# One VectorE call per convolution tap over all three thirds of the channels, in a kernel that fuses a seven-tap convolution with a GELU feed-forward block

## The chip, the cores and the metric

The kernel runs on one core of a Trainium2 chip. The metric is the device time of one execution in microseconds (us); the kernel before took 670.76 us in the median of three runs (670.53 to 673.35). TensorE (PE) multiplies matrices, VectorE (DVE) and ScalarE (ACT) do elementwise work, GpSimd (POOL) and SyncE (SP) mostly start transfers. Each engine has an instruction queue of its own and works it off in order. Between engines, and between two instructions of one engine that depend on each other, order is kept by semaphores only: an instruction adds to a semaphore when it has finished, and another waits until the semaphore has reached a number.

## The reference

The input is `x` of 8 x 4096 tokens with 192 channels. Each channel is convolved along the sequence with a causal filter of seven taps; the 24 channels of a head share a filter, which is a softmax over seven weights. The result goes through a feed-forward block of width 2048 with exact GELU:

```
out[b,s,h,g] = sum over k of softmax(weight[h])[k] * x_pad[b, s+k, h, g]      # 7 taps
h   = out @ w_in                        # 192 -> 2048
y   = gelu(h) @ w_out                   # 2048 -> 192
```

## The kernel before, in words

**Tiling.** The 32768 tokens are taken in two halves, which sit on partitions 0 to 63 and 64 to 127. Each half has 35 batches: six of 256 tokens, then 29 of 512 (`WS`). The 192 channels lie on 64 partitions in three *thirds*: channel 3i+p is row i of third p. So a convolution tap of a 512-token batch works on 128 partitions x 3 x 512 elements, that is 1536 a partition, and of a 256-token batch on 768.

**The way of batch n.** SP loads it into `xin`. VectorE transposes it into `xT` (`trans`, L729), channels on partitions. Then VectorE runs the taps: for each token, `acc = acc + x shifted by k * weight k` in float32 (`conv`, L757 scalar_tensor_tensor; tap 0 is a plain multiplication, L750), and the last tap writes bfloat16 into `xc`. Batches 0 and 1 (`PC`) get their convolution from TensorE instead. TensorE multiplies `xc` by `w_in` (`mm1`, L999) in 16 slices (8 for a 256-token batch), ScalarE puts GELU on each slice (L904) into `gT`, and TensorE multiplies that by `w_out` one batch later, between the slices of the next batch's `mm1` (L1077; L1143 in the batches named below). VectorE transposes the result into `osb` (L370, L537), and SP stores it.

**Calls of a tap.** Before the change each tap is two VectorE calls, s = 0 over the first two thirds (1024 elements) and s = 1 over the last third (512). Each tap reads what the tap before wrote. With two calls, the one that a call depends on is always the last but one on the queue, and the wait on `S_CV` is for that one (`idx - 1`).

**Batches in K0.** In most batches (4, 5, 6 and all from 9 on whose number less three is not in `ST`) ScalarE computes tap 0 in three instructions, one per third (`first_tap`, L872, 512 elements each). They are placed in ScalarE's queue before GELU slices 7, 10 and 12 of batch n-2 (`TAPS`; slices 2, 3 and 5 for batch 6). VectorE's first call of such a batch is tap 1, and each of its two calls waits on `S_K0` for the thirds that it reads.

**Batches in ST.** Every third batch from 9 to 33 (`ST`) has its second product computed by a scheme with fewer multiplications. It needs sums of GELU outputs (`st_add`: S1 at L473, S3 at L475, Dn at L478, S4 at L481), which VectorE makes while it convolves later batches, and combinations of the products (`st_post`, L510 to L525). TensorE's work for batch m in `ST` is a list of small units between the `mm1` slices of batch m+1 (`mm2_s`, L1143). The unit called P4 waits on `S_DP` for the first `st_post` call, here called *post0*: it subtracts what ScalarE has copied out, so that the bank can be accumulated into.

**The order on VectorE.** For each batch from 2 on `plan` lists its transpose and its conv calls, and the transpose of batch n+1 among them where that is a K0 batch. All other VectorE work (the sums, the post steps, the evacuations) is in a list `side` with a key (batch, position); a side operation goes out before the first plan operation whose position is not below its key. Positions count the calls of a tap, two each. For batch m in `ST`, the keys that matter here fall into batch m+2's list: S1 part 2 at position 1; S1 part 3, two evacuations, S3 and Dn at position 5; S4 at position 6; post0 at position 11. They come from these lines:

```
            "S1": [(1, 9, 0), (2, 0, 0), (2, 1, 0), (2, 5, -1)],
            "S3": [(2, 5, 1)],
            "Dn": [(2, 0, 2), (2, 5, 2)],
            "S4": [(2, 0, 4), (2, 6, 0)],
            "post": [(2, 11, 0), (3, 0, 0), (3, 2, 0), (3, 6, 0), (3, 9, 0)],
```

**Loads and buffers.** SP issues the load of a batch behind the store of an earlier one, which waits for three evacuations by VectorE. `xT`, `acc` and `xc` have two buffers each; GpSimd copies the six tokens of overlap between batches (`halo`, L652).

Of the kernel before, what the change touches and what calls it, by code (L numbers as in the profile page):

```python
# [11 lines left out]
def bass_lightweight_conv__then__act_gelu_exact_kernel(  # L12
# [8 lines left out]
    H, KS = weight.shape  # L21
# [7 lines left out]
    TB = 512  # L29
# [4 lines left out]
    PC = {0: 0, 1: 1}  # L34
# [5 lines left out]
    NP = D // 64  # L40
# [7 lines left out]
    HF = HX - (KS - 1)  # L48
    XW = HX + TB
# [69 lines left out]
    def ap(t, off, pat):  # L119
        return bass.AP(t, off, pat)  # L120

    with es:
# [52 lines left out]
        S_CV = sem("S_CV")  # L175
# [7 lines left out]
        S_K0 = sem("S_K0")  # L183
# [57 lines left out]
        def wait_pc(e, n, p):  # L241

            if n == 0:
                e.wait_ge(S_PCA, p + 1)
                if p >= 1:
                    e.wait_ge(S_PCE, p)
            else:
                e.wait_ge(S_PCA, len(PA) + 1)
                if p >= 1:
                    e.wait_ge(S_PCE, len(PV) + (0, 2, 5)[p])  # L250

        NCV = 2 * KS
        FQ = F // 8

        def part(q):
# [25 lines left out]

        def cvd(n):

            return sum(NCV - 2 * (m in K0) for m in range(n + 1) if m not in PC)


        def xin_at(n):
# [391 lines left out]
        @block.vector  # L679
        def _(v):  # L680
            v.memset(idb[:, :], 1.0).then_inc(S_MSET)
            v.wait_ge(S_WSB, 16)
            v.tensor_reduce(
                wmx[:, :], wsb[:, :], mybir.AxisListType.X, ALU.max, negate=True
            ).then_inc(S_PRO)
            v.wait_ge(S_ACTP, 2)
            v.tensor_scalar(wsm[:, :], wsm[:, :], 1e-9, None, ALU.add).then_inc(S_PRO)
            v.wait_ge(S_PRO, 2)
            v.reciprocal(wrc[:, :], wsm[:, :]).then_inc(S_PRO)
            v.wait_ge(S_PRO, 3)  # L690
            v.wait_ge(S_WNM, 1)
            v.tensor_scalar(  # L692
                wnm[0:H, 0:KS], wex[:, :], wrc[:, 0:1], None, ALU.mult
            ).then_inc(S_PRO)


            v.wait_ge(S_PRO, 4)
            v.transpose(wnt[:, :], wnm[:, :]).then_inc(S_PRO)
            v.wait_ge(S_PRO, 5)
            for q in range(4):  # L700
                v.transpose(  # L701
                    wcol[32 * q : 32 * q + 32, :],
                    ap(wnt, 4 * (q % 2), [[32, 32], [1, 4], [0, 8]]),
                ).then_inc(S_PRO)

            def trans(n, p):

                w = WS[n]
                if p == 0:
                    v.wait_ge(S_XP if n == 2 else S_XIN[n % NX], 64 if n == 2 else xin_at(n))  # L710
                    if n >= 2 and n - 2 in PC:
                        wait_pc(v, n - 2, NP - 1)
                    elif n >= 2:
                        v.wait_ge(S_CV, cvd(n - 2))
                    if n >= 2:
                        v.wait_ge(S_HALO, n)
                if n in PC:
                    out = ap(xT[n], p * XW + HX, [[NP * XW, 128], [1, w]])
                    src = ap(
                        xin[n % NX], p, [[TB // 32 * DQ, 128], [DQ, w // 32], [NP, 32]]  # L720
                    )
                else:
                    out = ap(xT[n % 2], HX, [[NP * XW, 128], [XW, NP], [1, w]])
                    src = ap(
                        xin[n % NX],
                        0,
                        [[TB // 32 * DQ, 128], [1, NP], [DQ, w // 32], [NP, 32]],
                    )
                v.transpose(out, src).then_inc(S_TR)  # L729

            def conv(n, k, s):

                w = WS[n]
                h = int(n in K0)
                p0, pn = (0, 2) if s == 0 else (2, 1)
                if k == h and s == 0:
                    v.wait_ge(S_TR, trd(n))
                if k == 1 and s == 0:
                    v.wait_ge(S_HALO, n + 1)
                idx = cvd(n - 1) + 2 * (k - h) + s  # L740
                kt = KS - 1 - k
                if k == h and h:
                    v.wait_ge(S_K0, NP * K0[n] + p0 + pn)
                elif idx >= 2:
                    v.wait_ge(S_CV, idx - 1)
                src = ap(xT[n % 2], p0 * XW + HF + kt, [[NP * XW, 128], [XW, pn], [1, w]])
                wk = wcol[:, kt : kt + 1]
                a = ap(acc[n % 2], p0 * TB, [[NP * TB, 128], [TB, pn], [1, w]])
                if k == 0:
                    ins = v.tensor_scalar(a, src, wk, None, ALU.mult)  # L750
                else:
                    dst = a
                    if k == KS - 1:
                        dst = ap(xc[n % 2], p0 * TB, [[NP * TB, 128], [TB, pn], [1, w]])
                        if n >= 2 and s == 0:
                            v.wait_ge(S_MM1, SL0[n - 1])
                    ins = v.scalar_tensor_tensor(  # L757
                        dst, src, wk, a, op0=ALU.mult, op1=ALU.add
                    )
                ins.then_inc(S_CV)  # L760

            plan = []
            for n in range(2, NB):
                ops = [] if n in K0 else [("t", n, 0)]
                ops += [("c", n, k, q) for k in range(int(n in K0), KS) for q in range(2)]
                if n + 1 in K0:
                    ops[6 if n < 6 else 2 : 6 if n < 6 else 2] = [("t", n + 1, 0)]
                plan.append(ops)  # L770

            def run(op):
                if op[0] == "t":
                    trans(*op[1:])
                else:
                    conv(*op[1:])

            trans(0, 0)
            for p in range(1, NP):
                trans(0, p)  # L780
            dup(v, 0, 0)
            for j in PV:
                conv_out(v, 0, j)
            dup(v, 1, 0)
            dup(v, 1, 1)
            trans(1, 0)
            trans(1, 1)
            trans(1, 2)
            dup(v, 2, 0)
            for j in range(1, 3):  # L790
                conv_out(v, 1, j)
            dup(v, 2, 1)
            for j in range(3, len(pieces(1))):
                conv_out(v, 1, j)

            side = [((M0 + 2, 4 * g, 0), evac, v, M0 - 1, g) for g in range(NG[M0 - 1])]
            side += [((M0 + 1, 2 * k + 1, 0), weights, v, k) for k in range(6)]
            for n in range(M0, M1):
                todo = []
                if n not in ST:  # L800
                    todo = [(at, evac_t, n, j) for j, at in enumerate(at_ev(n))]
                else:
                    for name, ats in AT_ST.items():
                        for q, at in enumerate(ats):
                            if name == "post":
                                todo.append((at, st_post, n, q))
                            elif name == "ev":
                                todo.append((at, st_evac, n, q))
                            else:
                                todo.append((at, st_add, n, name, q if name != "S3" else ND))  # L810
                side += [((n + at[0], *at[1:]), op, v, *rest) for at, op, *rest in todo]
            for n in range(M1, NB):
                for g in range(NG[n]):
                    side.append(((n + 3, g, 0), evac_half, v, g, 0))
            side.sort(key=lambda q: q[0])
            for b in range(2, NB):
                for o, op in enumerate(plan[b - 2]):
                    while side and side[0][0][:2] <= (b, o):
                        side[0][1](*side[0][2:])
                        side.pop(0)  # L820
                    run(op)
            for q in side:
                q[1](*q[2:])

# [93 lines left out]
        def _(t):  # L918
# [43 lines left out]
            def mm1(n, i):  # L962
# [6 lines left out]
                if i == 0:  # L969
                    if n in PC:  # L970
                        wait_pc(t, n, NP - 2)
                    else:
                        t.wait_ge(S_CV, cvd(n) - 1)
                if n == 0:
                    for j in {0: (0, 1), 2: (2, 5), 4: (3,), 6: (4,)}.get(i, ()):
                        t.wait_ge(S_WIN[j], 16)
# [6 lines left out]
                if head:  # L983
                    todo.sort(key=lambda q: q[1] == NP - 1)
                for cc, p in todo:
                    if i == 0 and cc == 0 and p == NP - 1:
                        if n in PC:
                            wait_pc(t, n, p)
                        else:
                            t.wait_ge(S_CV, cvd(n))  # L990
                    for hf in range(2):
                        r = slice(64 * hf, 64 * hf + 64)
                        ch = chunk(n, hf, i * c + cc)
# [259 lines left out]
```

## Time and profile before

| what | us |
|---|---|
| median of three runs | 670.76 (670.53 to 673.35) |
| profiled execution, first to last instruction (span) | 669.2 |
| what the median has on top of the span | 1.56 |
| TensorE busy | 665.8 (99%) |
| VectorE busy, 703 instructions | 604.7 (90%) |
| ScalarE busy, 659 instructions | 587.8 (88%) |
| GpSimd busy | 91.9 (14%) |

The profile gives no other time of the profiled execution than its span, so the span stands for it. Times in the timelines count from the start of the span. In a timeline a row gives the start, the length, the engine, the line, what is written and read, and how many like instructions are merged into it; a row can also say how long the engine sat idle before it and what ended that. From the first ST batch to the last the pattern repeats: in the timeline TensorE's rows return after 61.3 us, which is three batches.

### The profile page before, as it was taken

The page shows a single profiled execution, that of the slowest core. Times are in us where ns is not written, and L with a number is a line of the kernel's source. Part 1 is how long each engine was busy: PE and PEld are TensorE (multiplying, and loading weights), DVE is VectorE, ACT ScalarE, POOL GpSimd, SP SyncE. Part 2 cuts the span into 40 slices and gives each one's busy share as a digit, 9 for nine tenths or more (in the row PEclk, how much of TensorE's full clock was granted, in tenths as well). Part 3 has the DMA queues.
Part 4 walks back from the last instruction along what each step waited for, and adds up shares of the span by engine and source line. Part 5 has one row for each costly group of instructions (what it writes and reads, how often), then busy time and mean ns, then how long its engine had stood idle before and what let it go on. Part 6 is the DMA issues. An engine that isn't in the chain of part 4 may idle for free.

```text
span 669.2 us, 27224 instructions
## 1 busy us (share of the span) xinstructions
PE 665.8 (99%) x12504; PEld 416.2 (62%) x12504; DVE 604.7 (90%) x703; ACT 587.8 (88%) x659; POOL 91.9 (14%) x115
## 2 busy tenths in 40 slices
PE   9999999999999999999999999999999999999998
PEld 8999655556555655655565556556555655565567
DVE  5989999899999999999999999999999999999633
ACT  8999988899988988898999889888989998898783
POOL 8020000030012003001300120030013001200300
PEclk9999999999999999999999999999999999999999
DMA  9535234273466047515634660485157346602423
GB/s 153 123 86 132 61 72 97 73 132 85 96 143 139 9 96 176 112 36 126 140 84 97 140 143 7 96 176 111 39 127 140 82 97 142 139 8 61 119 63 96
DMA packets 142786, 67.82 MB, mean 101 GB/s; under 512 B 127248, under 2 KB 140880, under 8 KB 142672
## 3 DMA queue, kind: packets, MB, share of 16 engines
q1 hardware_dynamic: 129136, 49.37, 33.0%
q0 software_dynamic: 12416, 16.13, 12.1%
q8 instruction: 98, 1.61, 1.0%
q10 hardware_dynamic: 1120, 0.59, 0.3%
q14 instruction: 16, 0.13, 0.1%
HBM read 28.31 MB, written 25.17 MB: 80 GB/s over the span
## 4 chain that ended last, share of the span: by engine, by line
PE 99%; ACT 0%; DVE 0%; DMA 0%; issue 0%; ACTq 0%
PE hp L999 49%; PE ob L1077 29%; PE ob L1143 13%; PE ob L1039 5%; PE ob L1199 1%; PE hp L1199 1%; PE ob L941 0%; DMA wsb<-in_weight_dram 0%; PE ob L999 0%; ACT dg L846 0%; DVE wcol L701 0%; ACT xc L237 0%; DVE wnm L692 0%; ACT osb L344 0%; ACT wex L833 0%
## 5 line engine op out<-in xcount | busy, mean ns | idle before, releaser
L904 ACT ACTIVATE gT<-hp 128x1024 bf16<-128x1024 f32 x510 | 518.2, 1023 | 68.3 <-PE hp L999 60.5
L999 PE MATMUL hp<-xc,win 64*64 64x512 bf16 (+2 forms) x6036 | 416.8, 366 | 0.1
L757 DVE SCALAR_TENSOR_TENSOR acc<-xT,wcol,acc 128x1024 f32<-128x1024 f32 (+1 forms) x330 | 299.6, 957 | 7.3 <-ACT acc L872 7.3
L999 PEld LDWEIGHTS hp<-xc,win 64*64 64x64 bf16 (+1 forms) x6036 | 190.6, 106 | 126.5 <-ACT xc L237 0.3
L1077 PE MATMUL ob<-gT,wout 64*64 64x512 bf16 x3648 | 248.6, 376 | 0.0
L1077 PEld LDWEIGHTS ob<-gT,wout 64*64 64x64 bf16 x3648 | 116.9, 118 | 83.3
L1143 PE MATMUL ob<-gT,wout 64*64 64x512 bf16 x864 | 109.3, 376 | 0.0
L1143 PE MATMUL ob<-sst,wst 64*64 64x512 bf16 x432 | 88.9, 376 | 0.0
L729 DVE STREAM_TRANSPOSE xT<-xin 128x1536 f32<-128x1536 f32 (+2 forms) x39 | 74.6, 1922 | 9.7 <-DMA xin<-in_x_dram 9.3
L652 POOL COPY xT<-xT 128x18 f32<-128x18 f32 x30 | 28.9, 964 | 330.9 <-DVE xc L757 171.3
L1143 PEld LDWEIGHTS ob<-gT,wout 64*64 64x64 bf16 x864 | 48.8, 118 | 25.2
L757 DVE SCALAR_TENSOR_TENSOR xc<-xT,wcol,acc 128x1024 bf16<-128x1024 f32 (+1 forms) x66 | 61.9, 960 | 0.3
L370 DVE STREAM_TRANSPOSE osb<-ob 128x512 f32<-128x512 f32 x57 | 47.6, 874 | 4.0 <-PE ob L1077 3.7
L455 POOL DMA_DIRECT2D sst<-gT x27 | 19.8, 733 | 175.1 <-ACT gT L904 175.1
L872 ACT ACTIVATE acc<-xT,wcol 128x512 f32<-128x512 f32 (+1 forms) x63 | 43.6, 693 | 0.0
L1039 PE MATMUL ob<-wout,gT 64*128 64x192 bf16 x768 | 41.0, 243 | 0.0
L1143 PEld LDWEIGHTS ob<-sst,wst 64*64 64x64 bf16 x432 | 36.2, 107 | 6.0
L1143 PE MATMUL ob<-gT,wst 64*64 64x512 bf16 x144 | 39.7, 376 | 0.0
L1039 PEld LDWEIGHTS ob<-wout,gT 64*128 64x128 bf16 x768 | 33.4, 94 | 4.8
L458 POOL DMA_DIRECT2D sst<-gT x27 | 33.1, 1227 | 8.0 <-DMA sst<-gT 7.9
L473 DVE TENSOR_TENSOR sst<-gT 128x1024 bf16<-128x1024 bf16 x36 | 24.9, 691 | 10.0 <-ACT gT L904 9.9
L1143 PE MATMUL ob<-sst,wout 64*64 64x256 bf16 x288 | 30.8, 269 | 0.0
(75 smaller groups left out, 268.2 us busy)
## 6 DMA issues: line engine op xcount, KB each, us to landing
out_dram<-osb SPq DMA_DIRECT2D x124, 192.0 KB, 3.4
xin<-in_x_dram SPq DMA_DIRECT2D x116, 192.0 KB, 4.2
sst<-gT POOLq DMA_DIRECT2D x54, 256.0 KB, 4.1
xin<-in_x_dram SPq DMA_DIRECT2D x18, 96.0 KB, 2.4
wout<-in_moe_w_out_dram POOLq DMA_DIRECT2D x4, 192.0 KB, 4.5
win<-in_moe_w_in_dram POOLq DMA_DIRECT2D x4, 96.0 KB, 4.1
win<-in_moe_w_in_dram POOLq DMA_DIRECT2D x2, 192.0 KB, 4.1
xin<-in_x_dram POOLq DMA_DIRECT2D x4, 96.0 KB, 3.9
```

Source lines behind the costliest of these rows:

```text
L370: v.transpose(osb_t(m, j), bank(BK[m][j])).then_inc(S_EV)
L458: e.dma_start(dst, src, accum_op=ALU.add).then_inc(S_AD[q], 16)
L473: ins = v.tensor_tensor(t(0), a(1, 0), a(1, 1), ALU.add)
L652: g.tensor_copy(dst, src).then_inc(S_HALO)
L729: v.transpose(out, src).then_inc(S_TR)
L757: ins = v.scalar_tensor_tensor(dst, src, wk, a, op0=ALU.mult, op1=ALU.add)
L872: a.activation(out=acc[n % 2][:, p * TB : p * TB + w], in_=ap(xT[n % 2], p * XW + HX, [[NP * XW, 128], [1, w]]), func=AF.Copy, scale=wcol[ ...
L904: a.activation(out=ap(gT[n % 2], i * c * 2 * w, dst), in_=ap(ob, 2 * TB, [[4 * TB, 128], *src[1:]]) if u < SL0[1] and u % 3 == 2 else ap(h ...
L999: ins = t.matmul(hbuf(u, slice(fo, fo + fw), o, w), ap(win, f1, [[NP * F, 64], [2, fw]]), xc[n % 2][r, p * TB : p * TB + w], start=(p == 0 ...
L1039: ins = t.matmul(bb[sub], gT[m % 2][r, c0 : c0 + 128], wout[r, CH[sub][i] * C : (CH[sub][i] + 1) * C], start=(ph == 0 and k == 0), stop=(p ...
L1077: ins = t.matmul(bank(BK[m][j], slice(64 * h, 64 * h + 64), w), ap(wout, 64 * hf * NF * C + CH[h][i] * C + j, [[NF * C, 64], [NP, 64]],), ...
L1143: ins = t.matmul(bank(BK[m][bk], slice(64 * cg, 64 * cg + 64), w), wt_, a[r, c0 : c0 + w], start=(e == mine[0]), stop=(e in (mine[-1], GRO ...
```

## The change

A tap becomes one VectorE call over all three thirds: 1536 elements (768 in the 256-token batches). `S_CV` now counts one per tap, and a tap waits for the call just in front of it. In a K0 batch the first call waits for all three of ScalarE's thirds. TensorE's first matmul of a batch waits for all three thirds of `xc`, where before it waited for two and took the third up later. Positions in `plan` still count two per tap, so that the keys of the side list keep their meaning, but nothing can go out between the two halves of a tap any more.

```
-        NCV = 2 * KS
+        NCV = KS
...
-            def conv(n, k, s):
+            def conv(n, k):
...
-                p0, pn = (0, 2) if s == 0 else (2, 1)
...
-                idx = cvd(n - 1) + 2 * (k - h) + s
+                idx = cvd(n - 1) + k - h
                 kt = KS - 1 - k
                 if k == h and h:
-                    v.wait_ge(S_K0, NP * K0[n] + p0 + pn)
-                elif idx >= 2:
+                    v.wait_ge(S_K0, NP * (K0[n] + 1))
+                elif k == 0 and idx >= 2:
                     v.wait_ge(S_CV, idx - 1)
-                src = ap(xT[n % 2], p0 * XW + HF + kt, [[NP * XW, 128], [XW, pn], [1, w]])
+                elif k > 0:
+                    v.wait_ge(S_CV, idx)
+                src = ap(xT[n % 2], HF + kt, [[NP * XW, 128], [XW, NP], [1, w]])
...
-                ops += [("c", n, k, q) for k in range(int(n in K0), KS) for q in range(2)]
+                ops += [("c", n, k) for k in range(int(n in K0), KS)]
                 if n + 1 in K0:
-                    ops[6 if n < 6 else 2 : 6 if n < 6 else 2] = [("t", n + 1, 0)]
+                    at = 3 if n < 6 else 1 + (n not in K0)
+                    ops[at:at] = [("t", n + 1, 0)]
...
+                    o += 1 + (op[0] == "c")
...
-                        t.wait_ge(S_CV, cvd(n) - 1)
+                        t.wait_ge(S_CV, cvd(n))
...
-                    if i == 0 and cc == 0 and p == NP - 1:
-                        if n in PC:
-                            wait_pc(t, n, p)
-                        else:
-                            t.wait_ge(S_CV, cvd(n))
+                    if i == 0 and cc == 0 and p == NP - 1 and n in PC:
+                        wait_pc(t, n, p)
```

## The prediction

> **What bounds the kernel now.** I read the page first: the engines' busy time, then the chain that ended last.
>
> ```profile
> PE 665.8 (99%) x12504; PEld 416.2 (62%) x12504; DVE 604.7 (90%) x703; ACT 587.8 (88%) x659; POOL 91.9 (14%) x115
> ...
> PE 99%; ACT 0%; DVE 0%; DMA 0%; issue 0%; ACTq 0%
> ```
>
> TensorE is busy for 99% of the span and alone makes up the chain; the granted clock is 9 tenths or more in every slice. No VectorE time saved can shorten this. The change can only matter if VectorE hands something over so late that TensorE stops. So I next read the groups by shape, for the price of a call, and the waits.
>
> ```profile
> L757 DVE SCALAR_TENSOR_TENSOR acc<-xT,wcol,acc 128x1024 f32<-128x1024 f32 x145 | 184.1, 1270 | 0.0
> L757 DVE SCALAR_TENSOR_TENSOR acc<-xT,wcol,acc 128x512 f32<-128x512 f32 x165 | 122.3, 741 | 6.8 <-ACT acc L872 6.8
> ```
>
> ```profile
> DVE acc L757 <- ACT acc L872: 7.3, 12, 1.8
> ```
>
> The two shapes of a tap differ by 0.53 us for 512 elements. The small one has idle time before it: it waits for ScalarE's last third of tap 0, which the large one did not need. VectorE's timeline at the tightest place that I found, batch m+2 behind ST batch m:
>
> ```profile
> 324.57 1.26 DVE L757 SCALAR_TENSOR_TENSOR acc<-xT,wcol,acc 128x1024 f32<-128x1024 f32 x1
> 325.75 0.69 DVE L473 TENSOR_TENSOR sst<-gT 128x1024 bf16<-128x1024 bf16 x1
> 326.35 3.80 DVE L757 SCALAR_TENSOR_TENSOR acc<-xT,wcol,acc 128x512 f32<-128x512 f32 x4
> 330.41 0.69 DVE L473 TENSOR_TENSOR sst<-gT 128x1024 bf16<-128x1024 bf16 x1 [0.25 <-ACT gT L904]
> 331.01 1.60 DVE L370 STREAM_TRANSPOSE osb<-ob 128x512 f32<-128x512 f32 x2
> 332.48 0.66 DVE L475 TENSOR_TENSOR sst<-gT 128x1024 bf16<-128x1024 bf16 x1
> 333.05 1.22 DVE L478 TENSOR_TENSOR sst<-gT,sst 128x2048 bf16<-128x2048 bf16 x1
> 334.18 0.74 DVE L757 SCALAR_TENSOR_TENSOR acc<-xT,wcol,acc 128x512 f32<-128x512 f32 x1
> 334.84 1.22 DVE L481 TENSOR_TENSOR sst<-gT,sst 128x2048 bf16<-128x2048 bf16 x1
> 335.97 3.80 DVE L757 SCALAR_TENSOR_TENSOR acc<-xT,wcol,acc 128x1024 f32<-128x1024 f32 x4
> 339.69 1.28 DVE L757 SCALAR_TENSOR_TENSOR xc<-xT,wcol,acc 128x1024 bf16<-128x1024 f32 x1
> 341.00 0.69 DVE L510 TENSOR_TENSOR tq<-ob,p5s 64x512 f32<-64x512 f32 x1
> ```
>
> Here the first call starts at 324.57, and the last row, post0, ends at 341.69. ScalarE's timeline has the last third of tap 0 of this batch, and TensorE's weight loads have the P4 load that waits for post0:
>
> ```profile
> 325.31 0.71 ACT L872 ACTIVATE acc<-xT,wcol 128x512 f32<-128x512 f32 x1
> ```
>
> ```profile
> 342.52 0.11 PEld L1143 LDWEIGHTS ob<-gT,wst 64*64 64x64 bf16 x1
> ```
>
> That third ends at 326.02, 1.45 us after the first call has begun. P4's load is at 342.52, 0.83 us after post0. These two numbers decide the case: after the change the whole first tap waits for 326.02, and only 0.83 us lies between this stream and TensorE.
>
> **The change part by part.** *A call of 1536 elements.* By the two shapes in this window (1.28 and 0.75) it takes 1.28 + 0.53 = 1.81 us. The ends of calls overlap the next one's start: 324.57 to 325.75 is 1.18 for a call of 1.26, so a call is followed after its length less 0.08 by one that doesn't need it. In the four merged rows from 335.97 to 339.69 a pair takes 1.86. The new call takes 1.73 where a side operation follows. Where the next tap follows directly it waits for this one's end; the nearest rows for that:
>
> ```profile
> 282.21 2.29 DVE L729 STREAM_TRANSPOSE xT<-xin 128x1536 f32<-128x1536 f32 x1
> 284.54 0.75 DVE L750 TENSOR_SCALAR acc<-xT,wcol 128x1024 f32<-128x1024 f32 x1
> ...
> 320.76 0.69 DVE L473 TENSOR_TENSOR sst<-gT 128x1024 bf16<-128x1024 bf16 x1
> 321.55 1.23 DVE L478 TENSOR_TENSOR sst<-gT,sst 128x2048 bf16<-128x2048 bf16 x1
> ```
>
> A tap that reads the transpose's result starts 0.04 us after its end; a sum that waits for its predecessor and for GELU starts 0.10 after. A tap's wait that ends last is one, so I take 0.04: 1.84 per tap, against 1.86 for the pair. So 210 calls go, and VectorE's stream gains 0.13 us on a tap with something behind it and nothing on the others. Its busy time falls by some 20 us (210 x about 0.1); on the path this is worth 0.
>
> *The first tap's wait.* From 326.02 on, in the new order (nothing between the halves of a tap): 0.04 to the start of tap 1; 1.73 to S1 part 2; 0.60 (325.75 to 326.35) to tap 2; 1.84 to tap 3; 1.73 to S1 part 3, which is then at 331.96, later than its GELU; 0.61 (330.41 to 331.01), two evacuations 0.77 and 0.70 to 332.48, S3 0.57, so Dn starts 8.59 after 326.02. The half tap that stood between Dn and S4 is gone, so S4 waits for Dn: 1.22 + 0.10. Then 1.13 (334.84 to 335.97) to tap 4, 1.84 each to taps 5 and 6. Post0 came 0.03 behind the end of tap 6's first half (339.69 + 1.28 to 341.00), with its inputs there before, so I take 1.81 + 0.03, and its own 0.69. The sum is 17.25 us: post0 ends at 343.27 in place of 341.69. The shortest hand-over from VectorE to a weight load in the timeline of the head is 0.11, so the load is at 343.38, 0.86 late. A load begins one matmul (0.22) ahead of its matmul and takes 0.11, so about 0.11 stays hidden: TensorE stands for 0.75 us.
>
> ScalarE's third is tied to TensorE's pace, not to VectorE's, so this returns every period. It needs a batch m+2 behind an ST batch m: m = 9 to 30, eight times. **6.0 us.** Bounds from the same rows: with the overlap of 0.08 in place of the gap of 0.04 at the three direct successions, and of 0.10 at S4, the load is 0.54 less late, 0.21 a time, 1.7 in all; with 0.10 gaps throughout and nothing hidden, 1.04 a time, 8.3 in all. I take the row of the transpose, as its single late wait is the tap's.
>
> *In between.* S1 part 3 ends at 332.65; TensorE's load for it stood at 332.59. With the hand-over it is 0.17 late, of which 0.11 is hidden; this goes into the later stop of the same period, since VectorE isn't slowed by it. The evacuations of this batch come 1.55 us later with 1.77 to spare (their first ended at 331.90, TensorE's load was at 333.67), S4 0.9 later with 1.7 to spare.
>
> *The other K0 batch of a period* (m+1): its third was late before too (start 305.33, idle 0.35), and its transpose waited for a load until 307.25. Tap 1 runs from 305.33 to 307.14, no later; evacuations are 0.56 later with 3.7 to spare. The ST batch: its evacuation that starts store and load on SP's queue comes 0.5 earlier; so does the next load. GpSimd's halos and transfers wait for batches and GELU that don't move. Cost 0.
>
> *The wait for all three thirds at a batch's first matmul.* In the period `xc` is done 5 us or more ahead: 0. In the head the tightest was batch 2: the last third ended 0.61 us before its load; one 768-element chain (0.74 + 0.27 = 1.01 a call, 1.04 a tap against 1.06 a pair) ends 0.18 earlier, against a wait 0.19 earlier: 0. Batch 7's first thirds are 1.7 ahead of their load; its whole last tap ends 0.9 later than they did, since batch 6 starts at its late third: 0.
>
> *Batch 5, once.* Its taps start at the late third (45.02 in the timeline, not 43.80). Three taps at 1.04, 1.04 and 0.93 put the transpose of batch 6 from 47.54 to 48.03. ScalarE's next first-tap follows that transpose by 0.03, and TensorE has 0.05 at the tightest GELU behind it: **0.45 us**, between 0.2 (no gaps) and 0.5.
>
> **The sum.** 669.2 + 6.0 + 0.45 = 675.65 by the span; the median stands 1.56 above it, so 677.2, against 670.76.
>
> **Two rules weighed.** The Trainium skill's page DVE Perf Modes, section "The DRAIN you can't avoid", says that a semaphore between chained VectorE operations costs nothing extra; by that rule the taps follow as closely with the wait as without, and the sum is rival B. The 0.10 and 0.04 rows speak against it, the overlap of 0.08 in independent calls too. The page Perfetto Trace Analysis, section "Optimizing Scalar/DVE Operations", says that larger operations help where the engine is saturated, and that breaking instructions up lets work finish sooner where the engine isn't and makes others wait; VectorE's 58.5 busy us in a 61.3 us period (the table by stretches) lie near both, and by the first half alone it would be rival C.
>
> **The rivals.** *B, the chain of taps costs no gap.* The lower bounds: 670.76 + 1.7 + 0.2 = 672.7, within 0.5%. For it: a pair of taps leaves no gap now. Against: a pair always had a call between. Chance 0.13. *C, the other side: a call over three thirds is shorter than 1.81.* The six taps of the chain repay the 0.75 if each takes 0.125 less, so it decides at 1.685 us; there the kernel gives 670.8, and below that nothing more, since TensorE waits for nothing of VectorE now. Against: 0.53 for 512 elements leaves 0.22 fixed, and two thirds show no price for a second piece. Chance 0.05, of which 0.02 for a gain by something else. *D, longer gaps and nothing hidden:* 670.76 + 8.3 + 0.5 = 679.6; chance 0.12. The forecast has 0.70.
>
> **How the numbers follow.** 0.5% is 3.4 us, about what a measurement can tell from no change here: slower begins at 674.1. Forecast and D lie above, 0.82; B and most of C inside, 0.16; faster 0.02. The range goes from just under B to D, 672.4 to 679.8; the likeliest alone would be 675.5 to 679.
>
> **What would show it.** VectorE rows of L757 at 1.81 us with 1536 elements, each 0.04 behind the last. In batch m+2: tap 1 at 326.05 after idle time that ends with ScalarE's L872; post0 ending about 1.6 us later against it; in TensorE's rows eight stops of some 0.7 us before L1143 that end with DVE L510, and a period of 62.05 in place of 61.3. Wrong it would be if post0's lateness stayed under 0.9 us, or if those stops fell at another unit (S1 part 3, an evacuation).

## The result

The changed kernel is slower: 679.81 us in the median of four runs (677.69 to 682.11) against 671.12 us (four runs), a ratio of 1.0123 with a 95% interval of 1.0102 to 1.0144. (The ratios in this document are estimated from the single runs and differ a little from those of the medians, which give 1.0129 here.) A second comparison, with the last experiments below, gave 678.32 against 670.79 us, 1.0115 (1.0101 to 1.0129). In the first comparison two of the four executions were 4 us longer than the others and showed a mean granted clock of 0.997 in place of 1.000; no later execution showed that. The profiled execution took 677.69 us, its span 675.9, which is 6.7 over the span before.

The page of the changed kernel, busy times and the chain that ended last:

```profile
PE 667.7 (99%) x12504; PEld 480.5 (71%) x12504; DVE 596.4 (88%) x493; ACT 588.0 (87%) x659; POOL 76.5 (11%) x115
...
PE 69%; DVE 22%; issue 4%; ACT 3%; DMA 1%; POOL 1%; DVEq 0%; POOLq 0%
```

VectorE has 210 instructions fewer and is 8 us less busy, TensorE's busy time is about what it was, and yet VectorE now makes up 22% of the chain, where it had 0%. A busy share of 99% hides this: the page counts the few tenths of a us in which TensorE stands against 676. The waits (engine that waited, for whom, us in total, times, longest) name the place:

```profile
DVE acc L758 <- ACT acc L876: 34.6, 19, 3.2
...
PEld ob L1144 <- DVE tq L510: 7.8, 8, 1.0
...
PE ob L1144 <- DVE tq L510: 4.0, 8, 0.5
...
PEld ob L1144 <- DVE sst L473: 2.1, 7, 0.3
```

Lines from 757 on have moved by one and ScalarE's by four, so L758 is a tap, L876 ScalarE's tap 0, and L1144 the units behind an ST batch. VectorE waits 34.6 us for ScalarE where it waited 7.3. TensorE waits eight times for L510, which is post0, and seven times a little for L473, which is S1. Neither row existed before.

The two executions run the same 12504 matmuls in the same order, so each matmul's start can be set against its start before. The difference grows in steps, and between them stays as it is:

| where TensorE falls behind | us |
|---|---|
| up to batch 2 (this execution's head was earlier) | -0.43 |
| first matmul of batch 2, waits for `xc` | +0.07 |
| three GELU waits behind batch 5's late transpose | +0.63 |
| first matmul of batch 7, waits for `xc` | +0.27 |
| P4 behind ST batch 9, waits for post0 | +0.61 |
| the same behind batches 12 to 30, seven times about 0.73, each with 0.04 a little earlier | +5.4 |
| the last products | +0.20 |
| sum | 6.7 |

The eight stops are 6.0 us. VectorE's timeline of the changed kernel, batch m+2 behind the same ST batch as in the prediction:

```profile
326.09 1.23 DVE L481 TENSOR_TENSOR sst<-gT,sst 128x2048 bf16<-128x2048 bf16 x1
329.01 1.82 DVE L758 SCALAR_TENSOR_TENSOR acc<-xT,wcol,acc 128x1536 f32<-128x1536 f32 x1 [1.68 <-ACT acc L876]
330.75 0.69 DVE L473 TENSOR_TENSOR sst<-gT 128x1024 bf16<-128x1024 bf16 x1
331.35 3.66 DVE L758 SCALAR_TENSOR_TENSOR acc<-xT,wcol,acc 128x1536 f32<-128x1536 f32 x2
334.94 0.68 DVE L473 TENSOR_TENSOR sst<-gT 128x1024 bf16<-128x1024 bf16 x1
...
340.04 3.67 DVE L758 SCALAR_TENSOR_TENSOR acc<-xT,wcol,acc 128x1536 f32<-128x1536 f32 x2
343.74 1.82 DVE L758 SCALAR_TENSOR_TENSOR xc<-xT,wcol,acc 128x1536 bf16<-128x1536 f32 x1
345.59 0.69 DVE L510 TENSOR_TENSOR tq<-ob,p5s 64x512 f32<-64x512 f32 x1
```

and ScalarE's row of the third that it waits for, and TensorE's matmul that waits for post0:

```profile
328.17 0.71 ACT L876 ACTIVATE acc<-xT,wcol 128x512 f32<-128x512 f32 x1
```

```profile
346.34 0.40 PE L1144 MATMUL ob<-gT,wst 64*64 64x512 bf16 x1 [0.52 <-DVE tq L510]
```

VectorE sits idle for 1.68 us and starts tap 1 only when ScalarE's third is done (328.88). From there the stream runs without a hole to post0, which ends at 346.28, and P4 starts 0.06 later. The row's 0.52 us is the time in which no matmul ran at all; by the starts TensorE lost 0.73.

### The profile page after: what moved, and what is told of

The parts are those of the page before. It is cut to its first block, busy times and chain, and to the rows that moved or that the text cites. A ratio compares the mean times of both kernels' runs of the same rounds, so it can differ in the third digit from the quotient of the medians.

```text
span 675.9 us, 27014 instructions
## 1 busy us (share of the span) xinstructions
PE 667.7 (99%) x12504; PEld 480.5 (71%) x12504; DVE 596.4 (88%) x493; ACT 588.0 (87%) x659; POOL 76.5 (11%) x115
## 4 chain that ended last, share of the span: by engine, by line
PE 69%; DVE 22%; issue 4%; ACT 3%; DMA 1%; POOL 1%; DVEq 0%; POOLq 0%
PE hp L1000 34%; PE ob L1078 26%; DVE acc L758 14%; PE ob L1144 6%; ACT gT L908 2%; PE ob L1040 2%; DVE sst L481 1%; DVE sst L473 1%; DVE sst L478 1%; ACT acc L876 1%; DVE osb L370 1%; DVE tq L510 1%; PE ob L1200 1%; PE hp L1200 1%; DVE xT L729 1%
## 5 line engine op out<-in xcount | busy, mean ns | idle before, releaser
L1000 PE MATMUL hp<-xc,win 64*64 64x512 bf16 (+2 forms) x6036 | 501.9, 366 | 0.4 <-DVE xc L758 0.2
L1000 PEld LDWEIGHTS hp<-xc,win 64*64 64x64 bf16 (+1 forms) x6036 | 261.1, 106 | 95.7 <-ACT gT L908 1.2
L758 DVE SCALAR_TENSOR_TENSOR acc<-xT,wcol,acc 128x1536 f32<-128x1536 f32 (+1 forms) x165 | 281.4, 1706 | 36.9 <-ACT acc L876 34.6
L1078 PE MATMUL ob<-gT,wout 64*64 64x512 bf16 x3648 | 304.6, 376 | 0.0
L1078 PEld LDWEIGHTS ob<-gT,wout 64*64 64x64 bf16 x3648 | 168.8, 118 | 58.6
L1144 PE MATMUL ob<-gT,wout 64*64 64x512 bf16 x864 | 130.2, 378 | 0.0
L1144 PE MATMUL ob<-sst,wst 64*64 64x512 bf16 x432 | 91.1, 377 | 0.0
L1144 PEld LDWEIGHTS ob<-gT,wout 64*64 64x64 bf16 x864 | 62.6, 118 | 9.4
L758 DVE SCALAR_TENSOR_TENSOR xc<-xT,wcol,acc 128x1536 bf16<-128x1536 f32 (+1 forms) x33 | 56.8, 1720 | 1.1
L652 POOL COPY xT<-xT 128x18 f32<-128x18 f32 x30 | 13.6, 452 | 340.9 <-DVE xc L758 175.1
L876 ACT ACTIVATE acc<-xT,wcol 128x512 f32<-128x512 f32 (+1 forms) x63 | 43.7, 694 | 0.6 <-DVE xT L729 0.6
L1144 PE MATMUL ob<-gT,wst 64*64 64x512 bf16 x144 | 39.9, 377 | 4.0 <-DVE tq L510 4.0
L1144 PEld LDWEIGHTS ob<-sst,wst 64*64 64x64 bf16 x432 | 36.1, 107 | 9.8 <-DVE sst L473 2.1
L1144 PE MATMUL ob<-sst,wout 64*64 64x256 bf16 x288 | 32.3, 269 | 0.0
L473 DVE TENSOR_TENSOR sst<-gT 128x1024 bf16<-128x1024 bf16 x36 | 24.7, 685 | 7.0 <-ACT gT L908 7.0
```

The lines of the kernel that those rows point to most:

```text
L473: ins = v.tensor_tensor(t(0), a(1, 0), a(1, 1), ALU.add)
L758: ins = v.scalar_tensor_tensor(dst, src, wk, a, op0=ALU.mult, op1=ALU.add)
L876: a.activation(out=acc[n % 2][:, p * TB : p * TB + w], in_=ap(xT[n % 2], p * XW + HX, [[NP * XW, 128], [1, w]]), func=AF.Copy, scale=wcol[ ...
L1000: ins = t.matmul(hbuf(u, slice(fo, fo + fw), o, w), ap(win, f1, [[NP * F, 64], [2, fw]]), xc[n % 2][r, p * TB : p * TB + w], start=(p == 0 ...
L1078: ins = t.matmul(bank(BK[m][j], slice(64 * h, 64 * h + 64), w), ap(wout, 64 * hf * NF * C + CH[h][i] * C + j, [[NF * C, 64], [NP, 64]],), ...
L1144: ins = t.matmul(bank(BK[m][bk], slice(64 * cg, 64 * cg + 64), w), wt_, a[r, c0 : c0 + w], start=(e == mine[0]), stop=(e in (mine[-1], GRO ...
```

## The experiments

My theory was that of the prediction: the wait for ScalarE's last third, lengthened by the new order of the side operations, makes post0 late, and the loss is taken at P4. Rival 1 was that the wide calls and the gaps between dependent calls cost it, rival 2 that the single wait for all of `xc` at a batch's first matmul does.

**ScalarE's third one slice earlier, on the changed kernel.**

```
-        TAPS = (7, 10, 12)
+        TAPS = (7, 9, 11)
```

> The changed kernel with ScalarE's last two thirds of tap 0 placed before GELU slices 9 and 11 in place of 10 and 12 (one slice earlier, 1.29 us). My theory (the first tap waits for that third, and the chain behind it reaches P4 0.84 us late): the late load becomes 0.45 early, so the eight stops of 0.7 us before P4 go and so do the small ones at S1 part 3; what stays is the 0.9 us of the head. Time: before + 1 us, ratio 1.000 to 1.003. Rival 1 (wider calls and their gaps alone make TensorE late, wherever ScalarE's third is): the stops stay, before + 6 to 7, ratio 1.010. Rival 2 (the single wait for all three thirds at a batch's first matmul costs it): the stops stay and lie before L1000; ratio 1.010.

Measured: 672.19 us, ratio 1.0013 (1.0001 to 1.0026). Neither post0 nor S1 is among the things that TensorE waits for. The steps that are left are those of batch 5 (0.63) and batch 7 (0.26), and some in the first 18 us. Wide calls, gaps and the single wait at the first matmul are all still there, so they don't make the eight stops by themselves.

**The third one slice later, on the changed kernel.**

```
-        TAPS = (7, 10, 12)
+        TAPS = (7, 10, 13)
```

> The changed kernel with ScalarE's last third placed before GELU slice 13 in place of 12: the suspected wait lengthened by 1.29 us. My theory: each of the eight stops grows by 1.29 us (0.73 to 2.0), total before + 6.7 + 10.3 = 17, ratio 1.025. Rival 1 (calls and gaps, not the third): no change against the changed kernel, ratio 1.010. Rival 2: ratio 1.010, as xc is over 3 us ahead of its matmul.

Measured: 688.15 us, ratio 1.0249 (1.0233 to 1.0266). The total is as expected, but the added time does not lie where I said. The waits:

```profile
DVE acc L758 <- ACT acc L876: 48.9, 19, 4.1
...
PEld ob L1144 <- DVE sst L473: 12.5, 8, 1.6
...
PEld ob L1144 <- DVE tq L510: 7.9, 8, 1.0
```

Post0's row is that of the changed kernel. The 1.3 us are lost earlier, at the units that wait for S1 part 3 (steps of 1.17 once and 1.33 seven times), and TensorE, already late, then loses the same 0.7 at P4. At S1 part 3 my sum had no room left, only a stop of 0.06 us; a stream that is 1.3 us later meets it there first.

**Post0 ahead of tap 6, on the changed kernel.**

```
-            "post": [(2, 11, 0), (3, 0, 0), (3, 2, 0), (3, 6, 0), (3, 9, 0)],
+            "post": [(2, 9, 0), (3, 0, 0), (3, 2, 0), (3, 6, 0), (3, 9, 0)],
```

> The changed kernel with one key altered: post0 goes out before tap 6 of batch m+2 and not behind it. Late first tap, wide calls and gaps all stay. My theory (the loss is taken where P4 waits for post0): post0 ends some 1.8 us earlier, the eight stops at P4 go; the small ones at S1 part 3 (0.04 to 0.06) and the 0.9 us of the head stay. Before + 1.4, ratio 1.001 to 1.003. Rival 2 (the batch's first matmul waits for all of xc): nothing gained, as tap 6 ends 0.7 later: ratio 1.010 or more. A rival in which TensorE would then stop at the next late thing (an evacuation, S4, post1): a part of the 6 us comes back there.

Measured: 672.26 us, ratio 1.0009 (1.0000 to 1.0019). The waits still show the late third, in the same 19 places and up to the same 3.2 us (25.1 us in all), and S1:

```profile
DVE acc L758 <- ACT acc L876: 25.1, 19, 3.2
...
PEld ob L1144 <- DVE sst L473: 1.8, 7, 0.3
```

and no row of TensorE waiting for L510. The timeline has post0 ahead of the last tap:

```profile
338.38 3.67 DVE L758 SCALAR_TENSOR_TENSOR acc<-xT,wcol,acc 128x1536 f32<-128x1536 f32 x2
342.07 0.69 DVE L510 TENSOR_TENSOR tq<-ob,p5s 64x512 f32<-64x512 f32 x1
342.80 1.82 DVE L758 SCALAR_TENSOR_TENSOR xc<-xT,wcol,acc 128x1536 bf16<-128x1536 f32 x1
```

So, once the third is late, some 6 us hang on one subtraction of 0.69 us that stood behind a call of 1.82. Nothing else became late in its place. Rival 2 is out: tap 6, and with it `xc`, is later here than in the changed kernel relative to TensorE.

**The wait alone, on the kernel before.**

```
-                    v.wait_ge(S_K0, NP * K0[n] + p0 + pn)
+                    v.wait_ge(S_K0, NP * (K0[n] + 1))
```

> The kernel before, its two calls a tap kept, with one edit: the first call of a K0 batch waits for all three of ScalarE's thirds. My theory: from the third's end S1 part 3 starts 5.53 us later, post0 ends 16.8 later, which is 1.14 later than before, so P4's load is 0.43 late and TensorE stops 0.32 us, eight times: 2.6 us; and 0.6 once in the head behind batch 5. Before + 3.2, ratio 1.004 to 1.005. So the wait alone would be under half of the loss, and the rest the new order and gaps. Rival 1 (the calls' width and gaps): ratio 1.000. A theory that the wait alone is all of it: ratio 1.010.

Measured: 674.52 us, ratio 1.0046 (1.0030 to 1.0062). The steps at P4 are 0.28 us seven times, after 0.09 at the first; batch 5's is 0.77, and batch 7 loses 0.15. The waits have the same row at L510 (here TensorE's line is L1143):

```profile
PEld ob L1143 <- DVE tq L510: 4.3, 8, 0.6
```

So the wait alone makes about 2 of the 6.0 us at these stops, a third of them.

**The wait and the order, with two calls a tap, on the kernel before.** The same edit, and nothing of the side list goes out between the calls of a tap:

```
-                    while side and side[0][0][:2] <= (b, o):
+                    while side and side[0][0][:2] <= (b, o) and op[-1] != 1:
```

> The kernel before with its two calls a tap, but with the two other things that the change brings: the first call of a K0 batch waits for all three of ScalarE's thirds, and no side operation goes out between the two calls of a tap. My theory (the loss is the wait plus the order; a single call is itself shorter than the pair): the chain from the third's end to the end of post0 is 17.7 us, 0.44 longer than with single calls, so the eight stops are 1.2 us each; before + 10, ratio 1.015. The rival that the wide calls or the gaps between dependent calls cost the time: at most the 1.0046 of the wait alone, and in any case under the 1.010 of the changed kernel.

Measured: 680.91 us, ratio 1.0154 (1.0140 to 1.0168): more than with the change itself, in the same set of runs (1.0115). The steps of a period are 0.30 at S1 part 3 and 0.85 at P4, 1.16 together against 0.77. The waits:

```profile
PEld ob L1143 <- DVE tq L510: 9.0, 8, 1.1
...
PEld ob L1143 <- DVE sst L473: 4.3, 8, 0.6
```

This settles rival 1. The wide calls are not the cost: with the same wait and the same order, two calls a tap are 2.6 us slower over the kernel than one (680.76 to 682.16 against 677.71 to 679.94). The cost is the wait and the order. By the steps, the eight stops add up to about 2 us with the wait alone, 9 with the wait and the order, and 6.0 when the single call shortens the stream again.

**Tap 0 in another order, on the changed kernel.** In the changed kernel tap 0 on VectorE (L751) is a surprise. By shape:

```profile
L751 DVE TENSOR_SCALAR acc<-xT,wcol 128x1536 f32<-128x1536 f32 x10 | 18.1, 1812 | 0.3
```

Before the change its two calls took 0.753 and 0.462 us:

```profile
L750 DVE TENSOR_SCALAR acc<-xT,wcol 128x1024 f32<-128x1024 f32 x10 | 7.5, 753 | 0.3
...
L750 DVE TENSOR_SCALAR acc<-xT,wcol 128x512 f32<-128x512 f32 x12 | 5.5, 462 | 0.1
```

This edit walks the same elements, the halves of a third outermost:

```
-                    ins = v.tensor_scalar(a, src, wk, None, ALU.mult)
+                    ins = v.tensor_scalar(
+                        ap(acc[n % 2], 0, [[NP * TB, 128], [w // 2, 2], [TB, NP], [1, w // 2]]),
+                        ap(xT[n % 2], HF + kt, [[NP * XW, 128], [w // 2, 2], [XW, NP], [1, w // 2]]),
+                        wk, None, ALU.mult,
+                    )
```

> The changed kernel with tap 0 on VectorE walking the same 1536 elements in another order: outermost two halves of each third, then the three thirds, then 256 elements, so that the outermost count is even. In the changed kernel this call takes 1.81 us; the two calls before took 0.75 and 0.46, which gives 1.05 for the whole. If the odd outermost count of three is what costs it, 1.05 us comes back, and the 0.27 us that TensorE stands at batch 7 goes. If it is the length or the number of pieces, it stays at 1.81. Time: 0.3 below the changed kernel at most; the eight stops stay, since the late first taps lie in other batches.

```profile
L751 DVE TENSOR_SCALAR acc<-xT,wcol 128x1536 f32<-128x1536 f32 x10 | 10.2, 1021 | 0.3
```

The call takes 1.02 us, near the 1.05 expected, and the step at batch 7 is gone. The single run took 679.49 us; against the changed kernel that tells nothing of a few tenths. The eight stops are there as before (7.8 us of waiting for L510).

**Everything mended.** The changed kernel with `TAPS = (7, 9, 11)`, batch 5's thirds at slices 2, 4, 5, post0 ahead of tap 6, and tap 0 in the even order:

```
-        taps = {4: (3, 5, 6), 5: (3, 5, 6), 6: (2, 3, 5)}
+        taps = {4: (3, 5, 6), 5: (2, 4, 5), 6: (2, 3, 5)}
```

> The changed kernel with every stop that was found taken away: ScalarE's thirds before slices 7, 9, 11 (for batch 5 before slices 2, 4, 5), post0 before tap 6, tap 0 in the even order. My theory: nothing of the eight stops, of batch 5 and of batch 7 is left; before + 0 to 0.5, ratio 1.000 to 1.001, and not below the kernel before, whose TensorE already stood still for nothing of VectorE. If the saved VectorE time were worth anything once the stops are gone, the ratio would be below 0.998.

Measured: 670.76 us in the median of 11 runs, ratio 1.0000 (0.9991 to 1.0009). No step of 0.08 us or more is left after the first 13 us. The page:

```profile
PE 665.5 (99%) x12504; PEld 419.5 (63%) x12504; DVE 587.6 (88%) x493; ACT 587.2 (88%) x659; POOL 85.4 (13%) x115
...
PE 98%; DMA 1%; POOL 1%; DVE 0%; issue 0%; ACT 0%; POOLq 0%
```

VectorE does the taps in one call, is 17 us less busy than before, and the time is that of the kernel before. No version beat it.

**The changed kernel again.**

> The changed kernel unaltered, again, beside the following ones. All my terms: eight times 0.75 and 0.9 in the head and 0.2 at the end, 6.7 to 7 over the kernel before, ratio 1.010 (1.009 to 1.012). If the larger difference of the first comparison (8.7) belongs to the change and not to those executions, ratio 1.013.

Measured: 678.32 us, ratio 1.0115 (1.0101 to 1.0129), inside the 1.009 to 1.012 expected. Its eight stops add up to 6.0 us once more. Its profiled execution, the longest of the four at 679.94 us, is 1.34 us behind the kernel before when it comes to batch 2, where the first profile was 0.43 ahead, and it loses 0.52 at batch 2's first matmul: the transpose of batch 2 started 2.2 us later than in the first profile. In the profile of the kernel before, which waits for two thirds first, 0.6 to 0.8 us are to spare at that place; in the first profile of the changed kernel the tap that it waits for ended only 0.1 us ahead of TensorE's weight load. So it seems that in the changed kernel a late input transfer can cost TensorE time there; two profiles are not enough to show it.

## Why the prediction was right

The forecast was 677.2 us and slower, with a range of 672.4 to 679.8; the two comparisons gave 679.8 and 678.3. The first lies at the very edge of the range (its ratio, on the 670.76 us that the forecast started from, gives 679.0), the second well inside it. By its steps:

*The bound.* TensorE alone bounded the kernel, and saved VectorE time was worth 0. Shown by the mended kernel: the 17 us that VectorE saves leave the ratio at 1.0000.

*The call.* 1.81 us forecast; 1.80 (acc) and 1.82 (xc) measured by shape, so rival C's shorter call did not come:

```profile
L758 DVE SCALAR_TENSOR_TENSOR acc<-xT,wcol,acc 128x1536 f32<-128x1536 f32 x145 | 261.2, 1801 | 33.0 <-ACT acc L876 31.4
...
L758 DVE SCALAR_TENSOR_TENSOR xc<-xT,wcol,acc 128x1536 bf16<-128x1536 f32 x29 | 52.7, 1816 | 1.0
```

The gap to a dependent tap, 0.04 taken from the transpose's row, is 0.035 us in the median of the 93 places where tap follows tap. The mechanism of rival B, that a dependent tap follows as closely as an independent one, is out by the same rows: 0.035 behind the end, where a side operation starts 0.08 ahead of it. The Trainium skill's page VectorE: DVE Perf Modes, section "The DRAIN you can't avoid", on which the prediction weighed rival B, says that a semaphore between chained operations costs nothing extra; these 0.12 us per call are what it cost here.

*The first tap's wait and the chain to post0.* 17.25 us forecast from the third's end to post0's end; 328.88 to 346.28 is 17.40. Of the 0.15 more, 0.09 is the hand-over from ScalarE, 0.13 (328.88 to 329.01) and not 0.04. Three waits stand in front of this call. The hand-over was 0.13 in all 19 places of the changed kernel, and in the one place of the kernel before where a call with three waits waited for ScalarE (batch 5, at 43.80); the eleven calls there with one wait took 0.035.

*The stop.* 0.75 us forecast, eight times, 6.0; measured 0.61 once and 0.77 seven times, with S1 part 3's stop in it, 6.0 in both profiles. That it came so near is in part luck, because two more terms were off. The load that waits for post0:

```profile
346.34 0.10 PEld L1144 LDWEIGHTS ob<-gT,wst 64*64 64x64 bf16 x1 [1.00 <-DVE tq L510]
```

It starts 0.05 us behind post0's end, here and in the seven other places, where I took 0.11. Its matmul starts with it, at 346.34 too, so all of the 0.22 us by which a load else runs ahead stayed hidden, where I took 0.11. With the chain's 0.15 the load is 0.86 + 0.15 - 0.06 = 0.95 late, and less 0.22 that is 0.73. S1 part 3's small stop was forecast at 0.06 and came at 0.04.

*Batch 5.* 0.45 forecast; 0.63 measured, outside the range given (0.2 to 0.5). The transpose of batch 6 and ScalarE's tap behind it were late as forecast, with 0.05 us of room reckoned at the tightest GELU. The rows of the transpose, before and after:

```profile
47.54 2.27 DVE L729 STREAM_TRANSPOSE xT<-xin 128x1536 f32<-128x1536 f32 x1
```

```profile
47.81 2.26 DVE L729 STREAM_TRANSPOSE xT<-xin 128x1536 f32<-128x1536 f32 x1
```

TensorE was 0.36 us ahead of the kernel before at that point, so the transpose was 0.63 late against it, and not 0.49; 0.10 of the difference is again the hand-over of 0.13. TensorE lost as much in three steps, 0.26, 0.21 and 0.16: the 0.05 of room was hardly there.

*Batches 2 and 7.* Forecast at 0, measured 0.07 and 0.52 at batch 2, and 0.27 at batch 7. At batch 2 I set a chain that ends earlier against a wait that is earlier, and found them even, and I put nothing for a head that runs otherwise: in the first profile TensorE was early there, in the second the input of batch 2 came late. At batch 7 the step that failed is tap 0: I took 1.05 us from the two shapes before, and it was 1.81. The Trainium skill's page VectorE: DVE Perf Modes, section "Mode 2×_2P — use both read ports for one tensor", states a condition for two results a cycle: the outermost dimension that is not 1 has to be even, or odd and equal in source and destination. The source here is three rows of 512 with gaps, the destination one unbroken run of 1536. Our trace agrees: 1.81 us with three outermost, 1.02 with two, and in the 256-token batches, where source and destination both are three rows, 0.76 for 768 elements. I had not asked that of the one operation whose shape lost it.

*VectorE's busy time.* Some 20 us less forecast, 8 measured; with tap 0 in the even order it is 16 less (588.3), so tap 0 is most of the rest.

*The total.* 6.45 us by the span, 6.7 measured in the profiled execution. The medians stand 7.5 and 8.7 above, up to 2 us more than the terms. The second profile is 2.2 us longer than the first, and all of that lies in the head, up to batch 2's first matmul. What made the first comparison longer than the second stays unexplained.

## What to carry to other kernels

When one engine is busy 99% of the time, what another engine saves is worth nothing, and what it hands over too late makes the whole kernel longer; so cost such a change by its deadlines. Join two calls only after asking what stood between them and what the second half was waiting for: here a late input of one third came to hold back all of the tap, and a small operation with 0.8 us to spare came to stand behind a long one. And check that the joined shape keeps the rate of its parts.

## What I had not expected of the hardware

Two things. A float32 tensor-by-scalar call on VectorE took 1.81 us over 1536 elements when its source was three rows and its destination one run, and 1.02 us when the same elements were walked with an outermost count of two. And a longer wait did not deepen the stop at the last place but made a new one ahead of it: with the third 1.29 us later, TensorE's waits for post0 stayed at 7.9 us and those for S1 went from 2.1 to 12.5.
